# Reordering three instruction streams around the first product with w_out in a fused cross-attention and GELU kernel

## The chip, the cores and the metric

The kernel runs on one core of one Trainium2 chip. The metric is the device time of one execution in microseconds (us); the times given are medians over runs. A profile is one execution recorded by the hardware profiler. Its span runs from the first to the last instruction; the time of the same execution is a little longer. The engines of the core are PE (matrix products; PEld loads its stationary operand), ACT (functions such as exp and gelu, and copies), DVE (element-wise work), POOL (hardly used here) and SP (issues DMAs).

## The reference

Eight batches of cross-attention between 512 tokens and 32 state rows are computed (8 heads of 64), the two results are laid under each other, and a feed-forward block with a quick GELU runs over all of it.

```python
scores = scale * np.matmul(x, state.transpose(0, 1, 3, 2))
a = softmax(scores);  xread = np.matmul(a, state)
scores2 = scale * np.matmul(state, x.transpose(0, 1, 3, 2))
a2 = softmax(scores2);  sread = np.matmul(a2, x)
x = np.concatenate([xread, sread], axis=2)      # then (B*(S+Ns), 512)
h = x @ w_in                                    # 512 -> 2048
g = h * (1.0 / (1.0 + np.exp(-1.702 * h)))
out = g @ w_out                                 # 2048 -> 512
```

`softmax` stands here for the reference's own lines (maximum taken off, exp, divided by the sum with 1e-9 added). x, state and the output are float32; the weights come in as float64 and are rounded to float32 on the chip.

## The kernel before

The attention is folded into the weights: for each batch `M = state @ w_in` is made in four column parts (`att_M(b, c)`, 512 columns each), and the hidden layer is M times the transposed attention weights. One *up product* (`up_x(b, f)`, f from 0 to 15) gives 128 of the 2048 hidden columns for all 512 tokens: four passes on PE, 1.72 us, into one PSUM bank. A gelu on ACT takes the bank to SBUF. With `wait=True` the gelu is put on a list (`waiting`) and issued by a later `gelus(n)`; without it, it is issued at once.

**Rounding the weights.** The weights arrive in 32 pieces of 512 KB. Pieces 0 to 15 are w_in, pieces 16 to 31 are w_out, two for each of eight row blocks. For each piece DVE masks the exponent (L221), ACT turns it to a scale by two clamping activations (L232, L233), and DVE does sign, sum, fraction and product (L245, L258, L239, L264); pieces 18 and 19 have their clamps on DVE (L229, L230). A *round* is the DVE part, some 2.5 us with the mask of a piece ahead. `round_to(n)` does all rounds below n and issues masks and clamps two pieces ahead for w_out. A piece's room is loaded again when the piece four ahead of it is done, in SP's order. `nin` is 16.

**The order of the work.** The whole program is written out by hand: each engine runs its instructions in the order in which the code issues them, and a semaphore is waited for where data or a room demands it. The stages around the change are these.

1. *Up products of batches 0 and 1* (about 30 to 74 us), with the last rounds of w_in between them, then the maxima and exps of the state-side softmax (`two_s_max`, `two_s_exp`), the transposes of those exps (`att_eT`), and batch 0's late up products (`up_late`, f = 9 to 15), which take turns in the banks of the two-buffer pool `psH` and in four fixed banks `bank_o`.
2. *Batch 0's product with w_out*, by one level of Strassen's scheme (Winograd's form, seven products P1 to P7), as a loop over the eight row blocks i of w_out (L1553). A row block needs two rounded pieces, the sums of w_out (`pair_sums`: T1, t2, t4, B12) and, for even i, sums of batch 0's hidden columns (s1, s2, a21, s4). Each P is accumulated over the eight row blocks in a bank of its own: P1 in `bank_o[0]`. The eighth bank, `up_bank`, takes batch 1's up products f = 9 to 15, one in each row block from i = 2 on and one after the loop; f = 8 was made ahead of them and lies in `xn[0]` (`early`) until its room is free. Row block 0 also holds the state reads of batches 0 and 1 and the last two Ms of batch 1.
3. *After the loop* DVE adds up the results of P1 to P7 (L1616 to L1626), makes more sums and the turned x of batch 2, and ACT copies P1 to SBUF (k1) ahead of them.
4. *Batches 1 to 7* (`strassen_two`) run two levels of Strassen's scheme with small products (L802, eight passes, 0.89 us). Batch 1's first two products (P1, P2) are in one level (L851). Between them lies the attention of the next batch.

Of the kernel before, what the change touches and what calls it, by code (L numbers as in the profile page):

```python
# [20 lines left out]
def kernel(  # L21
# [30 lines left out]
    nc = tc.nc  # L52
# [7 lines left out]
    NG = H // NPR  # L60
# [6 lines left out]
    HF, HN = NF // 2, DM // 2  # L67
# [26 lines left out]
    def att_ps(shape, name):  # L94
        return psA.tile(shape, FP32, tag="att", name=name)
# [30 lines left out]
    bank_o = [psO.tile([P, FC], FP32, tag=f"o{i}", name=f"o_{i}") for i in range(4)]  # L126
# [151 lines left out]
    def powers_to(n):  # L278
        while done["a"] < min(n, len(PIECES)):
            load_weights(done["a"] + 1)  # L280
            round_a(done["a"])
            done["a"] += 1
# [5 lines left out]
    def round_to(n, ahead=AHEAD):  # L288

        nin = NFC * NPR  # L290
        while done["b"] < min(n, len(PIECES)):
            i = done["b"]
            powers_to(i + 1)
            round_b(i, min(i + 1 + ahead, i + 3 if i > nin + 3 else i + 2 if i >= nin else nin), i >= nin or i + 1 < nin and (i + 1 < n or i >= NPR))
            done["b"] += 1
            refill()
# [160 lines left out]
    def two_s_max(b):  # L457
        a = A[b]
        a["mx2"] = apool.tile([P, 2, NG], FP32, tag="mx4", name=f"mx4_{b}", bufs=2)
        mx = a["mx2"]  # L460
        for i in range(2):
            src = a["s"][i].rearrange("p (g t) -> p g t", g=NG)
            nc.vector.tensor_reduce(out=mx[:, i], in_=src, axis=AX.X, op=ALU.max, negate=True)
        nc.vector.tensor_tensor(out=mx[:, 0], in0=mx[:, 0], in1=mx[:, 1], op=ALU.min)
        nc.vector.tensor_scalar(mx[:, 0], mx[:, 0], scale, None, ALU.mult)

    def two_s_exp(b, room):
        a = A[b]
        sm = a["sm2"] = apool.tile([P, NG, 2], FP32, tag="sm4", name=f"sm4_{b}", bufs=2)
        a["e2"] = [(room[:, g], sm[:, g, :1]) for g in range(NG)]  # L470
        for g in range(NG):
            dst = room[:, g].rearrange("p (k i q) -> p k i q", k=2, i=2)
            for i in range(2):
                nc.scalar.activation(
                    out=dst[:, :, i], in_=a["s"][i][:, 2 * P * g : 2 * P * (g + 1)].rearrange("p (k q) -> p k q", k=2), func=AF.Exp,
                    bias=a["mx2"][:, 0, g : g + 1], scale=scale, accum_out=sm[:, g, i : i + 1],
                )
# [90 lines left out]
    def att_M(b, c, spare=False, banks=None, copied=True):  # L568

        m = mpool.tile([P, NG, FC], FP32, tag=f"M{turns['M'] % NFC if b < 2 else c}", name=f"M_{b}_{c}")  # L570
        turns["M"] += 1
        A[b]["M", c] = m
        name = f"M_{b}_{c}_"
        ps = banks or [
            psH.tile([P, FC], FP32, tag="h", name=name + str(g)) if spare else att_ps([P, FC], name + str(g)) for g in range(NG)
        ]
        by_state(b, ps, lambda rows, j: w_in[c][rows, j])
        M_banks[b, c] = ps
        if copied:
            M_copies(b, c)  # L580
# [56 lines left out]
    G = {}  # L637

    waiting = []

    def gelus(n):
        for _ in range(n):
            fn, kw = waiting.pop(0)
            fn(**kw)
# [19 lines left out]
    def up_x(b, f, spare=False, bank=None, wait=False, dst=None):  # L664
        c, o = divmod(P * f, FC)
        m = A[b]["M", c]
        up(b, f, S, [m[:, g, o : o + P] for g in range(NG)], [A[b]["aT"][:, g] for g in range(NG)], spare, bank, wait, dst)
# [623 lines left out]
    def rounds(n, *ahead):  # L1291
        round_to(done["b"] + n, *ahead)
# [92 lines left out]
    nin = NFC * NPR  # L1385
# [20 lines left out]
    up_four(0, 2 * nper)  # L1406
    powers_to(nin + 2)
    room = apool.tile([P, NPR, S], FP32, tag="xT", name="e2_01")
    two_s_max(1)
    two_s_exp(1, room[:, NG:])  # L1410
    rounds(1, 0)
    two_s_max(0)
    late_banks = [bank_o[2], None, bank_o[3], None, bank_o[0], bank_o[1], bank_o[2]]

    def up_late(f, wait=True):
        up_x(0, f, bank=late_banks[f - 2 * nper - 1], wait=wait)

    up_late(2 * nper + 1)
    up_late(2 * nper + 2)
    att_M(0, 3)  # L1420
    two_s_exp(0, room[:, :NG])
    up_late(2 * nper + 3)
    up_late(3 * nper)
# [47 lines left out]
    def four(t):  # L1471
        return t.rearrange("p a b -> p (a b)").rearrange("p (n t) -> p n t", t=HS)

    s_rooms = [
        four(mpool.tile([P, NG, FC], FP32, tag="M0", name="s_room")),
        four(apool.tile([P, NG, S], FP32, tag="aT", name="s2_room")),
    ]
    t_room = [pieces(mpool.tile([P, NG, FC], FP32, tag="M1", name="t_room_0"), 2, 2)]
    ps7 = {"P1": bank_o[0], "P6": bank_o[1], "P2": bank_o[2], "P5": bank_o[3]}
# [24 lines left out]
    def pair_sums(i):  # L1504

        f = ORDER[i]
        t2, t4 = t24(i)[:, 0], t24(i)[:, 1]
        steps = [
            (tt, v) for v in (
                (T1[:, f], B12[:, f], B11[:, f]), (t2, B22[:, f], T1[:, f]),  # L1510
                (t4, B21[:, f], t2), (B12[:, f], B22[:, f], B12[:, f]),
            )
        ]
        left = left_sums(i) if i % 2 == 0 else []
        if i == 0:
            first = left[:3]
            turns_of(first)
            turns_of(steps[:1] + left[3:] + steps[1:])
        else:
            turns_of([v for k in range(4) for v in left[k : k + 1] + steps[k : k + 1]])  # L1520

    def pair(i, *names):

        f = ORDER[i]
        a11, a12, a21, a22 = a_of(f)
        s1, s2, s4 = s_of(i) if i >= 0 and names[0] not in ("P1", "P2") else (None,) * 3
        t = t24(i) if s1 is not None else None
        for name in names:
            lhs, rhs = {
                "P1": lambda: (a11, B11[:, f]),  # L1530
                "P2": lambda: (a12, B21[:, f]),
                "P5": lambda: (s1, T1[:, f]),
                "P6": lambda: (s2, t[:, 0]),
                "P7": lambda: (a21, B12[:, f]),
                "P3": lambda: (s4, B22[:, f]),
                "P4": lambda: (a22, t[:, 1]),
            }[name]()
            for r in range(2):
                nc.tensor.matmul(  # L1539
                    ps7[name][:, HN * r : HN * (r + 1)], lhs[:, P * r : P * (r + 1)], rhs,  # L1540
                    start=(i == 0 and r == 0), stop=(i == HF - 1), skip_group_check=True,
                )
# [9 lines left out]
    rest = list(range(2 * nper, NF))  # L1552
    for i in range(HF):  # L1553
        round_to(nin + 2 * i + 2)
        if i == 0:
            pair(i, "P1")
            att_sread(1)
            att_M(1, 2, banks=bank_o[1::2])
            att_sread(0)
            att_M(1, 3, True)  # L1560
            pair(i, "P2")
            round_to(nin + 4)
            f_early = rest.pop(0)
            early = xn[0].rearrange("p h c d -> p (h c d)")[:, :S]
            up_x(1, f_early, dst=early)
            att_srT(0)
            att_srT(1)
            powers_to(nin + 6)
            t_room.append(pieces(apool.tile([P, NG, SCH * P], FP32, tag="eT", name="t_room_1"), 2, 2))
            s_rooms.append(four(apool.tile([P, NG, NB * Ns], FP32, tag="e1", name="s4_room")))  # L1570
            pair_sums(i)
            pair(i, "P6")
            ps7["P7"], ps7["P3"] = (psH.tile([P, FC], FP32, tag="h", name=f"down_{k}") for k in (7, 3))
            ps7["P4"], up_bank = (att_ps([P, FC], f"down_{k}") for k in (4, "up"))
        else:
            pair_sums(i)
            pair(i, "P1", "P2")
        if i == 2:
            G[1, f_early // 2] = free.pop(0)
        if i > 1 and i % 2 == 0:  # L1580
            up_x(1, rest.pop(0), bank=up_bank)
        if i == 2:
            nc.scalar.copy(G[1, f_early // 2][:, f_early % 2], early)
        late()
        if i > 1 and i % 2:
            up_x(1, rest.pop(0), bank=up_bank)
        if i == HF // 2 + 1:
            load_state(2)
            load_x_squares(2)
# [10 lines left out]
    room = away(6)  # L1600
# [3 lines left out]
    turns_of(s12_steps(0), s12_steps(1))  # L1604
    turn_x(2)

    k1, k2, t01, k3 = (s_rooms[i][:, 2 * j : 2 * j + 2] for i in (0, 2) for j in range(2))
    osb = opool.tile([P, 2, HN], FP32, tag="osb", name="osb_0_00")
    ps7 = {k: v.rearrange("p (r n) -> p r n", r=2) for k, v in ps7.items()}
    put = out_of(0)  # L1610
# [1 line left out]
    def put_out(i, k, src):  # L1612
        nc.sync.dma_start(put(slice(2 * i, 2 * i + 2), slice(HN * k, HN * (k + 1))), src)

    nc.scalar.copy(k1, ps7["P1"])
    tt(osb, ps7["P2"], k1, ALU.add)  # L1616
    put_out(0, 0, osb)
    tt(k2, ps7["P6"], k1, ALU.add)
# [6 lines left out]
    put_out(0, 1, t01)  # L1625
    tt(k3, ps7["P4"], k3, ALU.add)  # L1626
    put_out(1, 0, k3)
    for f, bank in zip(rest, (up_bank, bank_o[2])):
        up_x(1, f, bank=bank)
    for i, t in enumerate(t_room):  # L1630
        nc.scalar.copy(sums[:, 2, 2 * S * i : 2 * S * (i + 1)], t.rearrange("p n k t -> p (n k t)"))
    room = away(3)
# [97 lines left out]
```

## Time and profile before

| what | value |
|---|---|
| time, median of 3 runs | 691.59 us (691.44 to 691.82) |
| time of the profiled execution | 691.77 us |
| its span | 690.0 us |
| granted TensorE clock | 0.998 |
| HBM traffic | 68.94 MB read, 17.56 MB written |

The profile has several views. The first lists each engine's busy time. The chain of waits follows the work that ended last back to what released it. The list of waits says which engine stood idle for whom. A timeline gives instructions in order of time: start, duration, engine, line of the code, operation, what it writes and reads, how many are merged, and in brackets the idle time before it and what ended that. "PE h" is a bank of the pool `psH`, "PE o" one of `bank_o`, "down_up" is `up_bank`.

The stage of the change, in stretches (us from the start of the span): length, then busy time and number of instructions of PE, PEld, DVE, ACT and POOL, then the granted clock, the DMA share and GB/s.

```profile
60.00:75.00 15.00, 14.40 (x59) 6.69 (x58) 14.65 (x35) 14.61 (x35) 0.00 (x0) 1.00 0.30 103
75.00:83.00 8.00, 8.00 (x176) 4.63 (x175) 7.61 (x18) 5.41 (x13) 0.00 (x0) 1.00 0.21 73
83.00:138.00 55.00, 55.00 (x236) 44.66 (x236) 50.41 (x104) 18.80 (x31) 0.00 (x0) 1.00 0.39 114
138.00:143.00 5.00, 4.31 (x12) 1.98 (x11) 4.61 (x9) 1.68 (x4) 0.00 (x0) 1.00 0.44 174
143.00:159.00 16.00, 16.00 (x111) 12.18 (x110) 15.79 (x29) 6.89 (x10) 0.00 (x0) 1.00 0.49 171
159.00:168.00 9.00, 8.40 (x72) 8.00 (x72) 8.76 (x19) 2.85 (x10) 0.00 (x0) 1.00 0.76 215
```

### The profile page before, as it was taken

To read this page: it belongs to the slowest core of one execution; us is meant where nothing else is said; L and a number is where in the kernel's file an instruction comes from. 1 tells how busy PE (TensorE), PEld (TensorE's weight loads), DVE (VectorE), ACT (ScalarE), POOL (GpSimd) and SP (SyncE) were. 2 spreads that over 40 slices of the span, in tenths; PEclk is the share of its full clock that TensorE was granted. 3 is DMA by queue.
4 is the path that set the end of the run, shared out by engine and by line. 5 is a ranking of instruction groups with operands and counts; after the bars stand their busy time and mean duration, and the time that the engine had idled before them with its cause. 6 is when DMAs were issued, how large, how long until landed. Compare 5 with 4: busy or idle time off the path is not lost.

```text
span 690.0 us, 13614 instructions
## 1 busy us (share of the span) xinstructions
PE 678.1 (98%) x5355; PEld 578.6 (84%) x5355; DVE 558.5 (81%) x1066; ACT 326.6 (47%) x725; POOL 1.4 (0%) x10
## 2 busy tenths in 40 slices
PE   8999999999999999999999999999999999999996
PEld 4443687769999899889988998989988988999995
DVE  5999998999999886888969796888688885886540
ACT  7799823224355533662365435554375236421410
POOL 0000000000000000000000000000000000000000
PEclk9999999999999999999999999999999999999999
DMA  9731334337353664247443755175425640251000
GB/s 318 300 107 47 114 128 119 94 148 243 124 109 121 184 202 117 43 140 212 138 81 90 217 154 112 32 200 187 120 33 157 196 147 8 77 163 52 2 2 29
DMA packets 100159, 87.39 MB, mean 127 GB/s; under 512 B 56576, under 2 KB 79616, under 8 KB 100096
## 3 DMA queue, kind: packets, MB, share of 16 engines
q1 hardware_dynamic: 99552, 86.40, 42.1%
q8 instruction: 42, 0.69, 0.4%
q10 hardware_dynamic: 544, 0.13, 0.1%
q14 instruction: 21, 0.17, 0.1%
HBM read 68.94 MB, written 17.56 MB: 125 GB/s over the span
## 4 chain that ended last, share of the span: by engine, by line
PE 87%; DVE 6%; ACT 3%; DMA 2%; issue 0%; DVEq 0%; ACTq 0%
PE low L802 28%; PE o L1212 15%; PE o L802 15%; PE upx L1212 6%; PE o L1539 4%; PE M L430 3%; PE down L1539 3%; PE o L701 3%; PE upw L1212 2%; PE h L655 2%; PE down_up L655 1%; PE o L655 1%; PE sr L622 1%; PE o L430 1%; PE upx_sr L1212 1%; ACT low L233 1%
## 5 line engine op out<-in xcount | busy, mean ns | idle before, releaser
L802 PE MATMUL low<-w_out,g_room 128*128 128x128 f32 x416 | 54.3, 276 | 0.0
L802 PEld LDWEIGHTS low<-w_out,g_room 128*128 128x128 f32 x416 | 50.5, 192 | 4.5 <-issue 4.2
L1212 PE MATMUL o<-ta,M 128*128 128x256 f32 x192 | 49.9, 382 | 0.0
L1212 PE MATMUL upx<-aT,M 128*128 128x256 f32 x192 | 49.4, 380 | 0.0
L802 PE MATMUL low<-low,g_room 128*128 128x128 f32 x336 | 43.3, 275 | 0.0
L1212 PEld LDWEIGHTS o<-ta,M 128*128 128x128 f32 x192 | 35.5, 190 | 6.0 <-ACT g_room L1258 1.6
L802 PEld LDWEIGHTS low<-low,g_room 128*128 128x128 f32 x336 | 40.3, 192 | 0.0
L1212 PEld LDWEIGHTS upx<-aT,M 128*128 128x128 f32 x192 | 36.0, 190 | 4.7
L1218 ACT ACTIVATE g_room<-o 128x512 f32<-128x512 f32 (+1 forms) x56 | 31.3, 559 | 10.7 <-PE o L1212 10.7
L802 PE MATMUL low<-sums,later 128*128 128x128 f32 x272 | 34.9, 275 | 0.0
L566 ACT COPY M<-M 128x512 f32<-128x512 f32 x53 | 27.5, 596 | 13.9 <-PE M L430 13.9
L802 PEld LDWEIGHTS low<-sums,later 128*128 128x128 f32 x272 | 32.7, 192 | 0.1
L858 DVE TENSOR_TENSOR g_room<-g_room 128x512 f32<-128x512 f32 x48 | 31.8, 686 | 0.2
L1212 PE MATMUL o<-ta,ms 128*128 128x256 f32 x120 | 30.8, 379 | 0.0
L1258 ACT COPY g_room<-o 128x512 f32<-128x512 f32 (+1 forms) x28 | 15.5, 555 | 25.1 <-PE o L1212 25.1
L1218 ACT ACTIVATE g_room<-g_room 128x512 f32<-128x512 f32 (+1 forms) x28 | 16.8, 600 | 20.8 <-DVE g_room L1221 20.8
L1212 PEld LDWEIGHTS o<-ta,ms 128*128 128x128 f32 x120 | 22.8, 190 | 3.1
L1212 PE MATMUL o<-aT,m 128*128 128x256 f32 x96 | 24.6, 379 | 0.0
L802 PEld LDWEIGHTS o<-w_out,g_room 128*128 128x128 f32 x160 | 19.4, 192 | 5.0 <-issue 5.0
L232 ACT ACTIVATE low<-low,edge 128x512 f32<-128x512 int32 x30 | 21.7, 722 | 4.0 <-DVE low L221 3.9
L430 PE MATMUL M<-w_in,stT 64*32 64x512 f32 x344 | 23.2, 592 | 0.0
L858 DVE TENSOR_TENSOR g_room<-g_room,later 128x512 f32<-128x512 f32 x35 | 22.8, 684 | 0.0
(321 smaller groups left out, 1639.5 us busy)
## 6 DMA issues: line engine op xcount, KB each, us to landing
low<-low SPq DMA_DIRECT2D x108, 256.0 KB, 2.6
low<-low SPq DMA_DIRECT2D x11, 768.0 KB, 5.8
later<-in_moe_w_out_dram SPq DMA_DIRECT2D x16, 512.0 KB, 3.5
w_out<-in_moe_w_in_dram SPq DMA_DIRECT2D x12, 512.0 KB, 10.0
xsq<-in_x_dram SPq DMA_DIRECT2D x96, 64.0 KB, 2.1
xn<-in_x_dram SPq DMA_DIRECT2D x12, 512.0 KB, 4.0
out_dram<-osb SPq DMA_DIRECT2D x15, 256.0 KB, 2.2
out_dram<-later SPq DMA_DIRECT2D x14, 256.0 KB, 2.2
```

The lines of the kernel that those rows point to most:

```text
L232: nc.scalar.activation(out=sc.bitcast(FP32), in_=sc, func=AF.Relu, bias=edge[0], scale=-8.0)
L233: nc.scalar.activation(out=sc, in_=sc.bitcast(FP32), func=AF.Relu, bias=edge[1], scale=-1.0)
L430: nc.tensor.matmul(ps[g][st], state_of(b, NG * j + g, g), rhs(rows, j), start=True, stop=True)
L566: nc.scalar.copy(A[b]["M", c][:, g], ps)
L655: nc.tensor.matmul(hps, lhs[i], rhs[i], start=(i == 0), stop=(i == n - 1))
L701: nc.tensor.matmul(ps[:, r], lhs[f][:, P * r : P * (r + 1)], rhs[:, f], start=(first and r == 0 and f == 0), stop=(f == HF - 1), skip_grou ...
L802: nc.tensor.matmul(ps, lhs[f], rhs[:, f], start=(first and f == 0), stop=(f == QF - 1), skip_group_check=True)
L858: nc.vector.tensor_tensor(out=out, in0=x0, in1=x1, op=op)
L1212: nc.tensor.matmul(ps[:, k], lhs[i][:, o : o + P], rhs[i], start=(first and k == 0 and i == 0), stop=(i == n - 1), skip_group_check=True,)
L1218: nc.scalar.activation(out=dst, in_=src, func=AF.Gelu_apprx_sigmoid)
L1258: nc.scalar.copy(c12, Y(u))
L1539: nc.tensor.matmul(ps7[name][:, HN * r : HN * (r + 1)], lhs[:, P * r : P * (r + 1)], rhs, start=(i == 0 and r == 0), stop=(i == HF - 1), s ...
```

## The change

No computation is added or left out; instructions are issued in another order, and one product goes to another bank.

- *Before the loop:* the last round of w_in (`rounds(1, 0)`) comes ahead of batch 1's maximum, and `att_M(0, 3)` comes after the late up product f = 9 and ahead of the exps, where it came after f = 10 and between the exps of the two batches.
- *Row block 0:* `pair_sums(0)` comes ahead of the round of piece 19; the clamps of pieces 20 and 21 are issued after it, behind the gelu of f = 8 and the copies of the state reads.
- *Row blocks 2 to 7:* an up product's gelu is put on the list and issued at the start of the next row block, after that row block's rounds with the masks and clamps that they issue. The copy of f = 8 to its room moves from row block 2 to row block 3.
- *Row block 7 and after:* P1 is copied (k1) within the loop; f = 14 is written to `bank_o[0]`, P1's bank, and f = 15 to `up_bank`.

```diff
     room = apool.tile([P, NPR, S], FP32, tag="xT", name="e2_01")
+    rounds(1, 0)
     two_s_max(1)
-    two_s_exp(1, room[:, NG:])
-    rounds(1, 0)
-    two_s_max(0)
...
     up_late(2 * nper + 1)
+    att_M(0, 3)
+    two_s_exp(1, room[:, NG:])
+    two_s_max(0)
     up_late(2 * nper + 2)
-    att_M(0, 3)
     two_s_exp(0, room[:, :NG])
...
     for i in range(HF):
         round_to(nin + 2 * i + 2)
+        gelus(len(waiting))
+        if i == 3:
+            nc.scalar.copy(G[1, f_early // 2][:, f_early % 2], early)
         if i == 0:
...
             pair(i, "P2")
-            round_to(nin + 4)
             f_early = rest.pop(0)
...
             att_srT(1)
-            powers_to(nin + 6)
...
             pair_sums(i)
+            round_to(nin + 4)
+            powers_to(nin + 6)
             pair(i, "P6")
...
         if i > 1 and i % 2 == 0:
-            up_x(1, rest.pop(0), bank=up_bank)
-        if i == 2:
-            nc.scalar.copy(G[1, f_early // 2][:, f_early % 2], early)
+            up_x(1, rest.pop(0), bank=up_bank, wait=True)
+        if i == HF - 1:
+            k1 = s_rooms[0][:, :2]
+            nc.scalar.copy(k1, ps7["P1"].rearrange("p (r n) -> p r n", r=2))
         late()
         if i > 1 and i % 2:
-            up_x(1, rest.pop(0), bank=up_bank)
+            up_x(1, rest.pop(0), bank=up_bank if i < HF - 1 else bank_o[0], wait=True)
...
-    k1, k2, t01, k3 = (s_rooms[i][:, 2 * j : 2 * j + 2] for i in (0, 2) for j in range(2))
+    k2, t01, k3 = s_rooms[0][:, 2:], s_rooms[2][:, :2], s_rooms[2][:, 2:]
...
-    nc.scalar.copy(k1, ps7["P1"])
+    gelus(len(waiting))
     tt(osb, ps7["P2"], k1, ALU.add)
...
-    for f, bank in zip(rest, (up_bank, bank_o[2])):
-        up_x(1, f, bank=bank)
+    for f in rest:
+        up_x(1, f, bank=up_bank)
```

## The prediction

> **What bounds the kernel now.** I read the page's busy shares and chain first, then who waits for whom on PE, then the timelines of PE, ACT and DVE around each wait found.
>
> ```profile
> PE 678.1 (98%) x5355; PEld 578.6 (84%) x5355; DVE 558.5 (81%) x1066; ACT 326.6 (47%) x725; POOL 1.4 (0%) x10
> PE 87%; DVE 6%; ACT 3%; DMA 2%; issue 0%; DVEq 0%; ACTq 0%
> ```
>
> PE is the bound nearly everywhere. A change of order can win only where PE waits. Behind the start-up the list of waits has four entries for PE (us in total, times, longest):
>
> ```profile
> PE h L655 <- ACT M L566: 0.6, 1, 0.6
> PE down_up L655 <- ACT g_room L644: 0.7, 1, 0.7
> PE o L802 <- ACT o L811: 0.4, 1, 0.4
> PE o L802 <- DVE spare_M L807: 0.2, 1, 0.2
> ```
>
> These are modelled idle times; what a stall costs is read from starts, since four passes of an up product take 1.72 us (58.36 to 60.08) and eight small L802 ones 0.89. PE's timeline, at the four places:
>
> ```profile
> 61.89 1.51 PE L430 MATMUL M<-w_in,two 64*32 64x512 f32 x16
> 63.33 1.98 PE L655 MATMUL o<-aT,M 128*128 128x512 f32 x4
> 65.92 1.98 PE L655 MATMUL h<-aT,M 128*128 128x512 f32 x4 [0.60 <-ACT M L566]
> ...
> 137.80 1.88 PE L655 MATMUL down_up<-low,M 128*128 128x512 f32 x4
> 140.37 1.98 PE L655 MATMUL down_up<-low,M 128*128 128x512 f32 x4 [0.69 <-ACT g_room L644]
> ...
> 159.94 1.06 PE L802 MATMUL low<-low,spare_M 128*128 128x128 f32 x8
> 161.35 1.16 PE L802 MATMUL o<-low,spare_M 128*128 128x128 f32 x8 [0.36 <-ACT o L811]
> ...
> 164.14 1.06 PE L802 MATMUL low<-sums,spare_M 128*128 128x128 f32 x8
> 165.43 1.16 PE L802 MATMUL o<-low,later 128*128 128x128 f32 x8 [0.24 <-DVE spare_M L807]
> ```
>
> So the stalls are 65.92-63.33-1.72 = 0.87, 140.37-137.80-1.72 = 0.85, 161.35-159.94-0.89 = 0.52 and 165.43-164.14-0.89 = 0.40: 2.64 us in all. The chain of waits says where the last two come from: after the end of batch 0's product it leaves PE and runs on DVE for 24 us, fed by one copy on ACT:
>
> ```profile
> 137.97 1.73 PE down_up L655 x4
> 139.72 0.60 ACT g_room L644
> 140.32 0.48 ACT s_room L1615
> 140.83 0.69 DVE osb L1469
> ```
>
> The copy of P1 (L1615) needs a bank that was complete by 132.8 (its last product starts at 131.76), but it stands behind a gelu that waits for PE's late up product. And DVE reaches 140 late since, earlier, rounding of w_out waits for ACT, whose clamps (L232, L233) stand behind gelus of the same kind:
>
> ```profile
> 99.12 0.69 DVE L245 SCALAR_TENSOR_TENSOR low<-later,low 128x512 int32<-128x512 int32 x1 [1.34 <-ACT low L233]
> 110.67 0.69 DVE L245 SCALAR_TENSOR_TENSOR low<-later,low 128x512 int32<-128x512 int32 x1 [2.77 <-ACT low L233]
> ```
>
> **What the Trainium skill says.** "PSUM — Partial Sum Buffer", section "Engine vs sequencer instructions": ScalarE's and VectorE's queues are strictly first in, first out. The trace agrees: ACT sat idle 8.23 us before the gelu at 108.68 with clamps queued behind it. "ScalarE: Activation LUTs", section "What ACT_TABLE_LOAD costs", gives 1283 ns; here it is 1.28 (62.02, 68.34), and their number does not change. "Perfetto Trace Analysis", section "Identifying the Most-Contended Engine", warns that matmul busy share does not tell the distance to the limit; that is why I work from starts.
>
> **The change part by part.**
>
> *1. Batch 0's fourth M ahead of up product 10, the last round of w_in ahead of the first maximum.* PE's order becomes f8, f9, M, f10, f11, f12. Before, M (starts 61.89) was itself held: its last four weight loads came at 62.35, 0.74 after the last fraction step L264 started (61.61), and f11 followed 0.98 after that load. Now L245 follows the masks at 58.70 instead of 60.28, so L264 starts at 60.03, the last loads come at 60.77 and M ends at 61.75. f9 ends at 60.08, so M is held about 0.13 longer than before. Then f10, f11 take 3.44, and f12 starts at 65.19 instead of 65.92, if M's copies are done. ACT ends its clamps at 62.0, copies M by 63.0, and only then loads the exp table and does the eight exps: the same work in another order, so exps end at 68.2 and gelus begin at 69.64 as now. Cover of the copies at f12: 2.2 us. **Gain 0.73.**
> What next could be late: the transposes after f13 need the exps of batch 1 at 66.2 (PE there at 68.7); the second transpose bank needs f12's gelu, done 72.6 (PE 73.4). f15's bank needs f9's gelu, 70.2 (PE 71.3). All hold. The two maxima move on DVE from 58.69 and 62.22 to 60.7 and 62.2, ahead of exps that start at 64.3.
>
> *2. First row block's sums ahead of w_out's fourth piece.* DVE is free for them at 73.61 instead of 76.42. The eight sums cost 4.15 us as before. T1 writes the room that batch 1's state read still reads (PE ends it at 75.9), so DVE waits about 0.5 and ends near 78.4; the piece takes 2.8 (to 81.2). PE wants the sums at P6, now 81.9 (82.60 before). On PE nothing: **0**. But the gelu at L644 for f=8 now stands ahead of piece 20's clamps on ACT: gelu at 81.84, two small copies, the clamps end at 84.13 instead of 82.30. DVE's next round starts at 84.17 instead of 82.34, 1.83 late. What waits for it: P6 of row 2 at 95.7, for sums ready at 91.2. Hidden, with 4 us in hand.
>
> *3. Gelus behind the next clamps.* (A number in brackets is the round of that piece on DVE.) Masks and clamps no longer wait for PE's up products. DVE loses the idle 1.34 and 2.77: [24] starts at 99.53 (0.41 later than before), [26] at 108.3 (2.37 earlier), and by the end of batch 2's turns DVE is at 137.98 instead of 140.83. The price is a gelu behind up to four clamps (2.8 us). It matters where one bank serves two ups with only P1 and P2 (1.73 us) between them: f10 to f11, f12 to f13. f10 ends at 107.8; its four clamps need masks at 100.1 and 102.6, so they are over by 104.5; the gelu is immediate and done at 108.5, f11 begins at 109.5. Likewise f12 (clamps over by 119.7, product ends 123.3). The loads feeding the masks have 5.9 us between release and use, against 3.5 to landing. **0 on PE.** The early copy goes from row 2 to row 3 and is used only at the end: 0.
>
> *4. P1 copied in the loop, f14 into P1's bank.* The copy runs at about 132. f15 no longer waits for f14's gelu: **gain 0.85**. The next product into P1's bank starts at 140.5; f14's gelu is done at 139.4.
>
> *5. The DVE stretch behind it.* PE is now 0.73+0.85 = 1.58 earlier, DVE 2.85. The low product begins at 157.47; its third product could start at 159.26 and needs L811's copy. DVE's osb there ends at 158.1, ACT's exps (which move with PE) at 158.77, the copy ends near 158.9, PE can follow at about 159.1. Cover 0.15, thin. The last stalled product needs DVE's add, which comes at 162.26, PE at 162.84 less the 0.34 between add and product: cover 0.24. **Gain 0.52+0.40 = 0.92**, bounded by 0 below. From 165 on the trace has PE back to back and DVE busy to 187; DVE's lead (2.85) covers PE's shift (2.5), so the gain should reach the end.
>
> Queues: no DMA is added, and SP keeps its order; its weight loads and batch 2's x come earlier with DVE. POOL has nothing there.
>
> Sum: 0.73+0.85+0.92 = 2.50. The profiled execution took 691.77 us (span 690.0), so 689.27; the median of the runs is 0.18 lower than that execution: **689.1**.
>
> **The rivals.**
> *A. The thin covers fail.* Exps on ACT or the DVE chain arrive with PE, so the stalls at 161 and 165 stay or move: gain 1.58, 690.0. For: cover 0.15. Against: both feeders move by at least what PE does.
> *B. M's order brings little and the bank does:* ACT's exps collide with something behind, gain 0.85 at most, 690.7; that counts as no change. Against: ACT's work is the same and continuous from 62 to 75.
> *C. Slower: a gelu behind clamps holds the shared bank.* Place: f11 and f13. It decides if the masks of pieces 27 and 31 come over 4 us later than worked out (clamps over at 108.4 or later), say by late weight loads; every us beyond stops PE for one us, and a second hold only adds what DVE lost more. DVE 10 us late costs 6: 695. Against: the slack, and loads that have their queue to themselves then.
> *D. Nothing of the order does what it says.* The instruction order of the built kernel shows M's copies ahead of the exps, gelus behind clamps, and f14 in P1's bank; so this is out.
>
> **How the numbers follow.** Forecast (2.1 to 2.8 gained) 0.72; A 0.13; B or no change 0.07; C 0.08. Own range of the forecast: 688.8 to 689.5. With A and what B leaves, and 0.3 below for PE handing on small gaps I did not count (0.1 at the state read near 179): 688.5 to 690.4. About 0.2% (1.4 us) is what a measurement tells from no change: faster 0.85, within 0.07, slower 0.08.
>
> **What would show it.** Step 1: f12's start near 65.2 and no PE wait on L566. Step 2: DVE's T1 held by PE near 75.5. Step 3: ACT's long idles before gelus no longer end in a DVE wait for L233 at 99 and 110. Step 4: no PE wait on L644; DVE's osb near 138. Step 5: no PE wait on L811 or L807 between 157 and 165. Wrong would be any new PE wait on L644 at f11 or f13, or a stall that appears after 165.

## The result and the profile after

| | before | changed |
|---|---|---|
| time, median | 691.77 us (7 runs) | 689.84 us (688.99 to 690.46, 7 runs) |
| time of the profiled execution | 691.77 us | 688.99 us |
| its span | 690.0 us | 687.2 us |
| spans of all runs | 689.6 to 690.5, median 690.1 (85 runs, taken beside the experiments) | 687.1 to 687.6, median 687.2 |

The ratio of the times is 0.9969, with a 95% interval of 0.9958 to 0.9981: faster by 0.2 to 0.4%, or 1.3 to 2.9 us. The median span is 2.9 us shorter, but the median time only 1.9. Both numbers matter below, since they differ.

The busy shares and the chain, from the page of the changed kernel:

```profile
PE 677.6 (99%) x5355; PEld 578.7 (84%) x5355; DVE 558.0 (81%) x1066; ACT 327.9 (48%) x725; POOL 1.5 (0%) x10
PE 94%; DMA 2%; DVE 2%; ACT 1%; issue 0%; DVEq 0%; ACTq 0%
```

PE is as long busy as before; what went is the time in which it stood. The chain now runs through PE for 94% of the span instead of 87%: the stretch on DVE behind batch 0 is off it. The stretches show the same: PE was busy for 14.40 of the 15 us from 60 on, for 4.31 of the 5 from 138 on and for 8.40 of the 9 from 159 on, and it is busy for all of them now. Behind the start-up the list of waits has no entry for PE any more. PE's timeline at the four places (f9 to f13 at the top are batch 0's late up products, f14 and f15 below are batch 1's):

```profile
58.15 1.88 PE L655 MATMUL o<-aT,M 128*128 128x512 f32 x4
59.96 1.65 PE L430 MATMUL M<-w_in,two 64*32 64x512 f32 x16
61.54 1.98 PE L655 MATMUL h<-aT,M 128*128 128x512 f32 x4
63.36 1.88 PE L655 MATMUL o<-aT,M 128*128 128x512 f32 x4
65.08 1.88 PE L655 MATMUL h<-aT,M 128*128 128x512 f32 x4
66.79 1.88 PE L655 MATMUL o<-aT,M 128*128 128x512 f32 x4
...
136.86 1.88 PE L655 MATMUL o<-low,M 128*128 128x512 f32 x4
138.58 1.88 PE L655 MATMUL down_up<-low,M 128*128 128x512 f32 x4
140.29 3.62 PE L851 MATMUL o<-w_out,g_room 128*128 128x256 f32 x16
...
158.04 1.06 PE L802 MATMUL low<-low,spare_M 128*128 128x128 f32 x8
158.94 1.06 PE L802 MATMUL o<-low,spare_M 128*128 128x128 f32 x8
...
161.62 1.06 PE L802 MATMUL low<-sums,spare_M 128*128 128x128 f32 x8
162.57 1.16 PE L802 MATMUL o<-low,later 128*128 128x128 f32 x8
```

Batch 0's f12 (65.08) follows f11 without a gap, batch 1's f15 (138.58) follows f14 in 1.72, and the two small products follow in 0.90 and 0.95, against 1.41 and 1.29 before. From batch 0's f9 to f13 PE took 8.64 us (66.79-58.15) instead of 9.38 (67.74-58.36): 0.74 less. From f13 to batch 1's first product (L851) it took 73.50 instead of 74.45: 0.95 less. From there to the next product behind the last stall (starts 163.56, before 166.43) it took 23.27 instead of 24.24: 0.97 less. Together that is 2.66. Another 0.21 between these two traces lies ahead of f9, which the change doesn't touch; over all traces f9 starts between 57.97 and 58.45. Behind 166 the two traces are the same length within 0.1.

What fed this is seen on ACT and DVE of the changed kernel:

```profile
103.52 0.72 ACT L233 ACTIVATE low<-low,edge 128x512 int32<-128x512 f32 x1
107.74 0.60 ACT L644 ACTIVATE g_room<-down_up 128x512 f32<-128x512 f32 x1 [3.49 <-PE down_up L655]
...
131.88 0.59 ACT L1587 COPY s_room<-o 128x512 f32<-128x512 f32 x1 [4.58 <-PE o L1539]
```

```profile
83.97 0.69 DVE L245 SCALAR_TENSOR_TENSOR low<-later,low 128x512 int32<-128x512 int32 x1 [1.92 <-ACT low L233]
...
107.93 0.69 DVE L245 SCALAR_TENSOR_TENSOR low<-later,low 128x512 int32<-128x512 int32 x1
...
137.41 0.66 DVE L1469 TENSOR_TENSOR osb<-o,s_room 128x512 f32<-128x512 f32 x1
...
157.41 0.69 DVE L858 TENSOR_TENSOR osb<-o,g_room 128x512 f32<-128x512 f32 x1 [0.23 <-PE o L851]
...
162.22 0.29 DVE L807 TENSOR_TENSOR spare_M<-o,spare_M 128x128 f32<-128x128 f32 x1
```

The clamps are over (103.52+0.72) before the gelu of batch 1's f10 (107.74) has anything to do, and P1 is copied at 131.88. DVE waits for a clamp once (83.97) and not at 99 or 110 (the same rounds start at 99.23 and 107.93); it reaches osb at 137.41 (140.83 before), and at 157.41 it is DVE that waits for PE.

### The profile page after: what moved, and what is told of

The parts are those of the page before. It is cut to its first block, busy times and chain, and to the rows that moved or that the text cites. A ratio compares the mean times of both kernels' runs of the same rounds, so it can differ in the third digit from the quotient of the medians.

```text
span 687.2 us, 13616 instructions
## 1 busy us (share of the span) xinstructions
PE 677.6 (99%) x5355; PEld 578.7 (84%) x5355; DVE 558.0 (81%) x1066; ACT 327.9 (48%) x725; POOL 1.5 (0%) x10
## 4 chain that ended last, share of the span: by engine, by line
PE 94%; DMA 2%; DVE 2%; ACT 1%; issue 0%; DVEq 0%; ACTq 0%
PE low L802 28%; PE o L1212 15%; PE o L802 15%; PE upx L1212 6%; PE o L1539 4%; PE M L430 4%; PE down L1539 3%; PE o L655 3%; PE h L655 3%; PE o L701 3%; PE upw L1212 2%; PE o L851 2%; PE down_up L655 1%; PE o L430 1%; PE sr L622 1%; PE upx_sr L1212 1%
## 5 line engine op out<-in xcount | busy, mean ns | idle before, releaser
L858 DVE TENSOR_TENSOR g_room<-g_room 128x512 f32<-128x512 f32 x48 | 31.8, 686 | 0.2
L858 DVE TENSOR_TENSOR g_room<-g_room,later 128x512 f32<-128x512 f32 x35 | 22.8, 685 | 0.0
```

The source lines that it names most:

```text
L858: nc.vector.tensor_tensor(out=out, in0=x0, in1=x1, op=op)
```

## The experiments

All are edits of the changed kernel, but for one that is an edit of the kernel before. The numbers are summed up first; spans are medians over the runs. They were taken in three groups, and the kernel before, measured with each group, had median spans of 690.1, 690.05 and 690.0.

| what is altered | span, us | runs | against the changed kernel |
|---|---|---|---|
| changed kernel, first and second time | 687.2, 687.15 | 7, 6 | |
| M's order back | 687.9 | 6 | +0.7 |
| sums' place back | 687.1 | 5 | 0 |
| gelus at once | 688.7 | 20 | +1.5 |
| f14 in the shared bank | 688.1 | 11 | +0.9 |
| the same, P1 copied late | 689.2 | 20 | +2.0 |
| before, with bank and copy alone | 689.5 | 12 | +2.3 (-0.55 against the 36 runs of before in its group) |
| eight copies ahead of f10's gelu | 687.9 | 7 | +0.7 |
| fourteen copies | 694.9, 693.4 | 2 | +7.7, +6.2 |
| M one product later | 687.8 | 10 | +0.6 |
| the same, exp table loaded first | 686.7 | 5 | -0.5 |
| the same, sums' place back too | 686.6 | 5 | -0.6 |

### Taking the parts back, one by one

**M's order.**

```diff
-    rounds(1, 0)
     two_s_max(1)
+    two_s_exp(1, room[:, NG:])
+    rounds(1, 0)
+    two_s_max(0)
...
     up_late(2 * nper + 1)
-    att_M(0, 3)
-    two_s_exp(1, room[:, NG:])
-    two_s_max(0)
     up_late(2 * nper + 2)
+    att_M(0, 3)
     two_s_exp(0, room[:, :NG])
```

> The changed kernel with only the fourth M's order as before (M after f10 and between the exps, last w_in round behind the first maximum). If the gains add up stage by stage: PE waits on L566 again ahead of f12, from f9 to f13 9.38 us instead of 8.64, the span 0.7 longer (687.9), nothing else changed. If instead DVE sets the end of the stretch whatever PE does (rival): PE's loss is absorbed in the DVE stretch behind batch 0, the span stays at 687.2.

The span was 687.9, and PE's only wait is the old one. Its timeline:

```profile
58.13 1.88 PE L655 MATMUL o<-aT,M 128*128 128x512 f32 x4
...
63.10 1.98 PE L655 MATMUL o<-aT,M 128*128 128x512 f32 x4
65.69 1.98 PE L655 MATMUL h<-aT,M 128*128 128x512 f32 x4 [0.60 <-ACT M L566]
67.51 1.88 PE L655 MATMUL o<-aT,M 128*128 128x512 f32 x4
```

From f9 to f13 9.38 us, as expected, and the whole of it reaches the end. The rival falls.

**The sums of row block 0.**

```diff
             pair(i, "P2")
+            round_to(nin + 4)
             f_early = rest.pop(0)
...
             att_srT(1)
+            powers_to(nin + 6)
...
             pair_sums(i)
-            round_to(nin + 4)
-            powers_to(nin + 6)
```

> The changed kernel with the round of piece 19 and its successors' clamps ahead of row block 0's sums, as before. If the sums' place is worth nothing on PE: span 687.2 within 0.2, P6 of row 0 not held (sums ready about 79.6, PE there at 81.7), and DVE 1.9 us earlier from 84 on, since it no longer waits for the clamps behind the gelu of f8. Rival, the sums were needed early: PE stands at P6 or P7 of row 0 by up to 1 us, span 688.

The span was 687.1, without a wait of PE. DVE reached osb at 135.43 instead of 137.41, so it was 2 us earlier, and gave it all back waiting for PE. These are its waits in the stretch, in this kernel (who waited for whom, us in total, times, longest):

```profile
DVE e L455 <- PE o L430: 2.3, 1, 2.3
DVE osb L858 <- PE o L851: 0.2, 1, 0.2
```

So this part of the change is worth nothing in time, and costs DVE 2 us that nobody needs.

**The gelus behind the clamps.**

```diff
-            up_x(1, rest.pop(0), bank=up_bank, wait=True)
+            up_x(1, rest.pop(0), bank=up_bank)
+        if i == 2:
+            nc.scalar.copy(G[1, f_early // 2][:, f_early % 2], early)
...
-            up_x(1, rest.pop(0), bank=up_bank if i < HF - 1 else bank_o[0], wait=True)
+            up_x(1, rest.pop(0), bank=up_bank if i < HF - 1 else bank_o[0])
...
-        gelus(len(waiting))
-        if i == 3:
-            nc.scalar.copy(G[1, f_early // 2][:, f_early % 2], early)
```

> The changed kernel with each late gelu of batch 1 issued at once and the early copy back in row block 2; the copy of P1 in the loop and f14 in P1's bank stay. If DVE's lead is what removed the two stalls behind batch 0: DVE waits for L233 near 108 by 1.8 us, reaches osb near 139.2 instead of 137.4, and the waits on L811 and L807 come back with 1.0 to 1.5 us together, span 688.2 to 688.7. Rival, the early copy of P1 alone did it: span 687.2.

The span was 688.7, 1.5 longer. DVE waited for the clamps again, came to osb at 139.55, and both stalls were back on PE, the first larger than in the kernel before. The lines are DVE's wait and PE's timeline:

```profile
109.87 0.69 DVE L245 SCALAR_TENSOR_TENSOR low<-later,low 128x512 int32<-128x512 int32 x1 [1.73 <-ACT low L233]
...
158.18 1.06 PE L802 MATMUL low<-low,spare_M 128*128 128x128 f32 x8
160.04 1.16 PE L802 MATMUL o<-low,spare_M 128*128 128x128 f32 x8 [0.81 <-ACT o L811]
...
162.82 1.06 PE L802 MATMUL low<-sums,spare_M 128*128 128x128 f32 x8
164.11 1.16 PE L802 MATMUL o<-low,later 128*128 128x128 f32 x8 [0.24 <-DVE spare_M L807]
```

They cost 160.04-158.18-0.89 = 0.97 and 164.11-162.82-0.89 = 0.40. The early copy of P1 alone, which this kernel keeps, isn't enough.

**f14's bank, and the place of P1's copy.** First only the bank:

```diff
-            up_x(1, rest.pop(0), bank=up_bank if i < HF - 1 else bank_o[0], wait=True)
+            up_x(1, rest.pop(0), bank=up_bank, wait=True)
```

> The changed kernel with f14 in the shared bank again, ahead of f15; the copy of P1 stays in the loop. Own theory: f15 waits 0.85 for f14's gelu and its first product takes 0.1 longer, no other wait, span 688.1. Rival, PE's stall there was covered by the DVE stretch: span 687.2 to 687.4.

The span was 688.1, with one wait on PE: f15 started at 139.24 behind f14 at 136.68, so 2.56 for 1.72. Then the copy's place was taken back too:

```diff
-        if i == HF - 1:
-            k1 = s_rooms[0][:, :2]
-            nc.scalar.copy(k1, ps7["P1"].rearrange("p (r n) -> p r n", r=2))
...
     gelus(len(waiting))
+    k1 = s_rooms[0][:, :2]
+    nc.scalar.copy(k1, ps7["P1"])
     tt(osb, ps7["P2"], k1, ALU.add)
```

> The changed kernel with f14 in the shared bank and P1 copied after the loop, behind f14's gelu. Own theory: DVE's osb waits for the copy until 139.8 (137.4 in the changed kernel), PE is 0.95 later, so DVE is 1.0 short behind batch 1's P2 and the waits on L811 and L807 come back with about 1.0, span 689.2. Rival, the place of the copy is of no account once DVE doesn't wait for clamps: span 688.1, like the run with the shared bank alone.

The span was 689.2, 1.1 more. DVE, early as it was, stood for the copy, and the stalls on L811 and L807 were back with 0.51 and 0.40 (the latter product started at 164.74):

```profile
140.15 0.69 DVE L1469 TENSOR_TENSOR osb<-o,s_room 128x512 f32<-128x512 f32 x1 [2.40 <-ACT s_room L1618]
```

So the last two stalls need both: a DVE that isn't held by clamps, and a copy that doesn't hold it at the end.

**Bank and copy alone, on the kernel before.** The edit of the kernel before:

```diff
+        if i == HF - 1:
+            k1 = s_rooms[0][:, :2]
+            nc.scalar.copy(k1, ps7["P1"].rearrange("p (r n) -> p r n", r=2))
         late()
         if i > 1 and i % 2:
-            up_x(1, rest.pop(0), bank=up_bank)
+            up_x(1, rest.pop(0), bank=up_bank if i < HF - 1 else bank_o[0])
...
-    nc.scalar.copy(k1, ps7["P1"])
```

> The kernel before with only the copy of P1 in the loop and f14 in P1's bank. Own theory: PE saves 0.95 at f15, but DVE, whose chain sets PE's time at 165, is only 0.4 earlier (osb at 140.4 instead of 140.8), so the waits on L811 and L807 grow by 0.55 and the span falls by 0.4 only, to 689.6. Rival, each stall is worth its own length: span 689.05 or less.

The span fell by 0.55 to 689.5, near the 0.4 expected, though the stall at f15 was gone. DVE's osb and PE's small products of this kernel:

```profile
140.10 0.65 DVE L1469 TENSOR_TENSOR osb<-o,s_room 128x512 f32<-128x512 f32 x1
...
158.72 1.06 PE L802 MATMUL low<-low,spare_M 128*128 128x128 f32 x8
160.58 1.16 PE L802 MATMUL o<-low,spare_M 128*128 128x128 f32 x8 [0.80 <-ACT o L811]
...
164.65 1.16 PE L802 MATMUL o<-low,later 128*128 128x128 f32 x8 [0.24 <-DVE spare_M L807]
```

What PE saved at f15 it lost behind it: the two stalls cost 0.97 and 0.40, 1.37 where the kernel before has 0.92. The 0.85 of a stall on PE is not its worth while another engine's chain decides a little later.

That DVE's chain decides here can be read from the starts. From DVE's osb (L1469) to PE's product behind L807 it is 24.60 us in the kernel before (140.83 to 165.43), 24.56 with the gelus at once (139.55 to 164.11), 24.59 with the copy late (140.15 to 164.74) and 24.55 here (140.10 to 164.65), though PE came to batch 1's first product (L851) at times up to 1.8 us apart (140.43 to 142.19). In the changed kernel it is 25.16 (137.41 to 162.57).

### Making the suspected cost larger

The rival in the prediction that made the kernel slower was a gelu behind too much work on ACT. Copies that write the same values again were put in its way, in row block 4:

```diff
+        if i == 4:
+            for _ in range(8):
+                nc.scalar.copy(G[1, f_early // 2][:, f_early % 2], early)
         gelus(len(waiting))
```

> The changed kernel with the early copy repeated eight times on ACT in row block 4, between the clamps of pieces 26 and 27 and the gelu of f10 (same values written; 3.9 us more on ACT). Own theory: the clamps are over at 104.2, f10 ends at 107.7 and f11 starts at 109.5, so a gelu behind 3.9 us is done at 108.7 and nothing is held, span 687.2. Rival, the gelu behind clamps is on the edge already: a PE wait on L644 at f11, up to 3.9 us more.

The span was 0.7 longer, which neither theory had expected: it is too much for the author's own, and too little for a gelu on the edge. The eight copies took not 3.9 but 5.06 us. They all write one place and come 0.63 apart, where M's two copies to different places come 0.48 apart:

```profile
104.19 5.15 ACT L1557 COPY g_room<-xn 128x512 f32<-128x512 f32 x8
109.25 0.59 ACT L644 ACTIVATE g_room<-down_up 128x512 f32<-128x512 f32 x1
```

```profile
108.45 1.03 PE L1539 MATMUL o<-w_out,sums 128*128 128x256 f32 x4
109.90 1.98 PE L655 MATMUL down_up<-low,M 128*128 128x512 f32 x4 [0.43 <-ACT g_room L644]
```

The gelu ends at 109.84 and f11, due at 109.31, starts at 109.90, 0.59 late. So the hold begins at some 4.5 us of extra work (5.06-0.59), and with the longer first product behind a wait (0.10) it shows as 0.7 of span. The mechanism is there, with some 4.5 us of room in the changed kernel. Then fourteen copies:

> The same with fourteen copies (6.75 us more on ACT). Own theory: ACT is through at 111.0, the gelu of f10 ends at 111.5, f11 is held by 2.1 us, and as PE is the bound from there on the span is 2.1 to 2.3 longer: 689.4. Rival, a hold there is absorbed by the lead of the other engines: span below 688.

Both theories missed. The hold was 4.48 us, which fits the 4.5 us of room, as ACT's copies took 8.97. But the span grew by 6.2 in one execution and by 7.7 in the other. The stretches of the latter, the one with a trace, tell why (length, then busy time of PE, PEld, DVE, ACT and POOL, clock, DMA share, GB/s):

```profile
109.00:113.80 4.80, 0.48 (x3) 0.08 (x1) 4.76 (x11) 4.61 (x9) 0.00 (x0) 0.90 0.43 137
113.80:117.00 3.20, 3.19 (x4) 1.51 (x5) 2.63 (x7) 2.63 (x4) 0.00 (x0) 0.50 0.79 205
117.00:121.00 4.00, 4.00 (x13) 3.01 (x12) 4.00 (x9) 3.27 (x5) 0.00 (x0) 0.66 0.78 127
```

While PE stood, its granted clock fell to a half: f11 took 3.58 instead of 1.82, the next two products 2.86 instead of 1.73, 2.9 us in all. If the clock is 1.00 or 0.50 and nothing between, a mean of 0.90 over 4.8 us is 1.0 us of half clock, and 0.66 over 4 us is 2.7. By this estimate the half clock stood from about 112.8, 3.5 us after PE's last product ended (109.32), to about 119.7, 5.9 us after PE went on. The Trainium skill, "TensorE: Matmul & The Clock Gate", section "What's actually happening", tells of such a gate: half clock after at least one idle window of about 3.4 us, full clock after at least one busy window of the same length. The fall agrees with that; the return took longer than one such window. The stalls under 1 us of the other runs left the clock at 1.00 in their stretches. Why the other execution lost 1.5 us less isn't shown, as it left no trace.

### Towards a better version

M is still held by w_in's last round in the changed kernel (59.96 to 61.54). One product later it isn't:

```diff
     up_late(2 * nper + 1)
+    up_late(2 * nper + 2)
     att_M(0, 3)
     two_s_exp(1, room[:, NG:])
     two_s_max(0)
-    up_late(2 * nper + 2)
```

> The changed kernel with the fourth M one product later (after f10), its copies still ahead of the exps. M is then not held by the last w_in round (0.55 on PE), but its copies end 1.05 later on ACT, and all exps and gelus with them. Own theory: ACT is the bound from 62 to 75, so f15 and the second transpose of batch 0 wait for gelus, and the span is 0.2 to 0.6 longer than the changed kernel's: 687.6. Rival, ACT has room there: span 686.7.

The span was 687.8, 0.6 longer, as the author's own theory had it. ACT stood 1.07 for M before it could copy it, all exps and gelus moved with the copies, and batch 0's f15 waited for f9's gelu:

```profile
71.57 1.98 PE L655 MATMUL o<-aT,M 128*128 128x512 f32 x4 [0.57 <-ACT sums L644]
```

With the load of the exp table in that gap on ACT:

```diff
     up_late(2 * nper + 2)
+    nc.scalar.activation(out=one, in_=one, func=AF.Exp)
     att_M(0, 3)
```

> As the run before, with an exp of one column ahead of M's copies on ACT, so that the load of the exp table fills the time in which ACT would wait for M. Own theory: copies end at 64.1, exps start where they do in the changed kernel (64.1) or 0.2 later, M isn't held: span 0.4 to 0.55 shorter than the changed kernel's, 686.7. Rival, the copies' end at 64.1 holds f12 or the later gelus hold f15: span 687.2 or more.

The span was 686.7, 0.5 shorter than the changed kernel (686.5 to 686.7 in five runs, where the changed kernel had 686.9 to 687.6 in thirteen); the time was 688.50, 0.9951 of the kernel before (0.9937 to 0.9965). ACT has no gap there, and M takes PE 1.02 instead of 1.58:

```profile
61.84 1.28 ACT L1418 ACT_TABLE_LOAD   x1
63.13 0.20 ACT L1418 ACTIVATE one<-one 128x1 f32<-128x1 f32 x1
63.24 1.05 ACT L566 COPY M<-M 128x512 f32<-128x512 f32 x2
64.18 0.52 ACT L474 ACTIVATE e<-sums,mx 128x256 f32<-128x256 f32 x1
```

```profile
61.68 1.09 PE L430 MATMUL M<-w_in,two 64*32 64x512 f32 x16
62.70 1.98 PE L655 MATMUL o<-aT,M 128*128 128x512 f32 x4
```

And with the sums' place taken back as well (both diffs are shown above):

> As the run before, and row block 0's sums back behind the round of piece 19, so that DVE is 1.9 us earlier from 84 on. Own theory: PE's gain of 0.4 to 0.55 needs DVE as much earlier, of which the changed kernel had only some 0.2 at batch 1's P2 to spare; with the lead back nothing of it is lost: span 686.6. Rival, DVE waits for PE there anyway: same as the run before.

The span was 686.6 and the time 688.47, a ratio of 0.9954 (0.9942 to 0.9967): no different from the run before. The rival holds; DVE needs no more lead.

## Why the prediction was right, and where it was off

- *Step 1, M's order:* 0.73 forecast, 0.74 measured in PE's timeline, 0.7 when taken back. The longer hold of M, forecast as 0.13, is 0.14 (1.58 against 1.44). That the sum is so close is in part luck. The first up product behind M takes 1.82 instead of 1.72 in the changed kernel too (61.54 to 63.36), so 0.10 of the stall of 0.87 could not be gained; and in the kernel before f12, the first product behind the wait, also took 1.82 (65.92 to 67.74), a cost of 0.10 that the sum left out. The two cancel.
- *Step 2, the sums:* 0 on PE, as forecast. The clamps behind f8's gelu made DVE wait till 83.97; 84.17 was forecast, and the whole trace begins 0.2 earlier. Wrong was the wait of T1: it started at 75.41, not near 76, while the state read ran to 75.7. T1's first slice lies over one head only, which is read in the first half; the forecast took the whole room. Nothing hung on it.
- *Step 3, gelus behind clamps:* 0 where they stand, and DVE at osb at 137.41 against 137.98 forecast, 0.2 of it from the start. No gelu held f11 or f13. The copies showed the room to be 4.5 us on ACT; the 4 us of the rival were about right. Its 6 us for 10 us of lateness left out the clock, and would be too few if that much lateness came; only the copies on ACT were tried, not late masks.
- *Step 4, f14's bank:* 0.85 forecast, 0.95 measured. Each restart after a wait costs 0.10 more: the first product of four passes takes 1.82 instead of 1.72 (140.37 to 142.19 in the kernel before). That term wasn't in the sum.
- *Step 5, the DVE stretch:* 0.92 forecast, 0.97 measured. The cover of 0.15 held at L811. At L807 the cover of 0.24 did not: 0.06 of a gap (0.95 for 0.89) and a restart of 0.10 are left, and what hides them in the sum are the two restarts that it had not counted as a gain (0.52+0.40+0.20-0.16 = 0.96). The add of L807 starts 4.81 after DVE's osb of L858, before as now (160.28 to 165.09, 157.41 to 162.22), and that osb now waits for PE's own product. So more lead of DVE can't close the gap: with the sums' place back, DVE 2 us earlier, the two starts are still 0.95 apart (161.74, 162.69). That both the clamps and the copy had to go was the forecast's reading of the chain, and the two runs that undo one of them show it.
- *The sum:* 2.50 was forecast; 2.66 was found on PE, and the median span fell by 2.9. The rest isn't located; spans of one kernel scatter by up to 0.9.
- *The one term that was mis-sized* is the last: "the profiled execution took 691.77 us (span 690.0), so 689.27" carries the 1.77 us outside the span over unchanged. They weren't the same. Over 85 runs of the kernel before they were 1.74 to 2.08; over 13 runs of the changed kernel they were 1.74 to 3.53, with a median of 2.7. So the profiled execution came in at 688.99, and the median only at 689.84. That is 0.74 above the forecast: outside the range of the forecast alone (688.8 to 689.5), inside the wider one (688.5 to 690.4), which was made wide for rival A and not for this. By the time alone one would have taken rival A (690.0) to be true; that the stalls at L811 and L807 were gone is seen only in the trace and the span.

The cause of that spread is open. The changed kernel was measured a second time with the expectation that it had as much time outside the span as the kernel before; it had 1.76 to 3.53 us again. The spread goes with one thing in these runs: in 98 runs of the kernels that have M's copies ahead of the exps, 35 had over 2.2 us outside the span; in the 18 runs with M's old order (six of the kernel with all other parts of the change, twelve of that with bank and copy alone) and in the 85 of before, none had over 2.08. Nothing in the span's records shows why, and six and twelve runs are few. A count over labels isn't a cause.

## What to carry to other kernels

Where PE is busy 98% of the span, look for the few places where it isn't, take their cost from the starts of neighbouring products, and ask for each whether PE's own queue or another engine's chain decides there: a stall of 0.85 us was worth 0.55 alone, since a DVE chain ended later. An engine with idle time is best made late or early by what stands ahead in its queue: work that waits for PE (a gelu) goes behind work that another engine waits for (a clamp), as far as the bank that it frees allows. A load of a function table fitted into a gap that a wait left on ACT, since a tiny instruction called for it there. And where gains are under 1 us, read them from spans beside times.

## What the runs showed of the hardware that was not expected

- A wait of PE cost 0.10 us more than its length: the first product behind it took 1.82 instead of 1.72, or 0.99 instead of 0.89. The first up product behind M (64x32 tiles) took 1.82 as well, without a wait (61.54 to 63.36; 62.70 to 64.52 where M wasn't held).
- Copies on ACT that write one place again and again came 0.63 us apart; two to different places 0.48. The repeated ones read SBUF and the two read PSUM, but that isn't the difference: two copies from SBUF to different places (L1635) took 1.99 for two of 1.04, so they overlapped by some 0.1 too (M's: 1.05 for two of 0.57).
- In a stand of PE of 4.5 us the granted clock fell to 0.50, and it stayed there for some 5.9 us after PE went on (estimated from the means of the stretches above); 2.9 us were lost. In the stretches with stands under 1 us, in the other runs, it was 1.00.
- The change to another function table cost its load and no more: in the changed kernel the exps' last record ends at 68.14, the load starts at 68.15 and takes 1.28, and the gelu starts at 69.45.
- The time outside the span isn't a constant: it was up to 3.55 us in the edited kernels, where it had been 1.8 (at most 2.08) in the kernel before.
